# Spreading the MLP's last product evenly over the attention units, and normalising three last units in the core

## The chip, the cores and the metric

The kernel runs on one core of a Trainium2 chip. The metric is the device time of one execution, in microseconds (us). Three executions of the kernel before took 214.60, 214.85 and 216.46 us; their median is 214.85 us. The profiled execution is another one: it took 215.85 us, of which 214.1 us lie between the first and the last recorded instruction (its span).

## What is computed

`x` has 2048 rows (positions) of 512 numbers, bf16. `xn` is its layer norm. Two branches start from it and meet in the last line:

```python
qkv = xn @ wqkv                       # 32 heads of width 16
# position s attends to s, s-2, ..., s-14 (8 keys, dilation 2)
s = softmax_over_8_keys(q . k / 4) @ v, heads joined, @ wo
h  = gelu(xn @ w1)                    # 512 -> 512
hs = shifted(h) @ w2                  # four column groups, shifted by +-1 and +-2 positions
x1 = xn + hs
h2 = gelu(layernorm(x1) @ w3) @ w4    # 512 -> 1376 -> 512
out = x + s * silu(x1 + h2)
```

## The kernel before, in words

Even and odd positions never attend to each other, so the rows are held as two parities `p` of 1024 rows each, in chunks `c` (0 to 3) of 512 rows and tiles of 128 rows. All engines work in the order of the source: a loop at the end of the function ties each instruction behind the one before it on its engine. So what stands late in the source waits for all that stands before it on the same engine.

**First half (up to about 107 us of the trace): the dense products.** `qk`, `w1`, `w2`, `w3` are done chunk by chunk in pairs of accumulator banks that go round the tags x, y, z (`psa`, L102). `w2(c)` (L336) makes four tiles in two halves; each half is evicted by VectorE (L348), which adds it onto `xn`. `stats(c, j, "l3")` (L208: L213, L214) takes mean and variance of one tile. `second_norm(c)` (L352) does that for the four tiles of a chunk and then `rstd` on GpSimd (L218, L219). `second_columns(c)` (L359) normalises (L229), writes the chunk to DRAM (L363) and reads it back transposed (L365) as the operand of `w3(c)` (L370, matmuls on L380).

**Second half: 17 attention units** (`order`, L56). Unit 0 takes the first rows of both parities, units 1 to 8 go through parity 0 and 9 to 16 through parity 1, 120 new rows each. Iteration `n` of the loop on L759 does, on TensorE: `scores(n)` (L556: 8 mask matmuls, 32 small ones), `weighted(n-1)` (L597: 64 small ones), `values(n+1)` (L535: 4 matmuls), in most iterations one tile of the MLP's last product, `w4_part` (L490: 11 matmuls, accumulated in bank w), and from n = 6 on one output tile, `final` (L728: 4 matmuls with `wo`). Which iterations have a `w4` tile is told by

```python
w4_at = {n: k for k, n in enumerate([*range(13), 14])}
```

so iterations 13 and 15 have none; the tiles 14 and 15 are done behind the loop (L791, L805). ScalarE makes the exponentials (L583) and copies the values (L550). VectorE copies the sums of a unit out of the accumulator (L625, L631, L632).

**Normalising.** `weighted` gives the weighted sums and, in extra columns, the denominators. Units are joined to runs (L59): unit 0 alone, pairs (1,2) to (13,14), then 15 and 16 alone, R = 10 runs. There are two ways to divide:

- *Through DRAM* (runs 0 to 7): `sums_out` (L640) sends the denominators to a small tile (`dn`, two DMAs on SP's queue, L649) and the sums to `oT`, transposed by head (eight DMAs on GpSimd's queue, L656). Two iterations later `sums_invert` (L699) takes the reciprocal (VectorE, L704) and writes it to DRAM (SP, L706), and `sums_read` (L709) reads it back spread over partitions (SP, L712), behind a wait for the write. One iteration after that, `sums_apply` (L715, VectorE L720) multiplies.
- *In the core* (the last two runs, units 15 and 16): four of the eight DMAs of `oT` go on SP's queue and four on GpSimd's. `sums_turn` (L661) transposes the denominators by 8 matmuls (L666), `sums_inverse` (L669) takes the reciprocal (VectorE, L674) and spreads it (ScalarE, L677), `sums_back` (L682) turns it back by 4 matmuls (L688), `sums_mult` (L694, VectorE L697) multiplies `oT`.

**Accumulator banks.** `layout` (L88) closes all pools of banks and opens new ones. It is called three times: for the dense products (L106), for the attention (L488: s = 4 banks for scores, o = 2, w = 1, b = 1) and behind the last unit (L793: f, g, h, i in place of s; o, w and b again). The first matmul into a newly opened bank waits for the last readers of what was closed with it.

**The end** (L783 to L814): scores and weights of the last unit, the two runs that are normalised in the core, `w4` tiles 14 and 15, and the output tiles 2 to 7 of parity 1. `final` multiplies the product by the gate on VectorE (L742, L744) and adds `x` on GpSimd, or on VectorE for the two last (L745); the last tile is done in two halves that are stored on two queues (L747).

Of the kernel before, what the change touches and what calls it, by code (L numbers as in the profile page):

```python
# [9 lines left out]
ALU = mybir.AluOpType  # L10
# [5 lines left out]
def kernel(  # L16
# [13 lines left out]
    pe, dve, act, pool, sp = nc.tensor, nc.vector, nc.scalar, nc.gpsimd, nc.sync  # L30
# [8 lines left out]
    NF = (F + P - 1) // P  # L39
# [5 lines left out]
    TPC = CH // P  # L45
# [10 lines left out]
    order = [(None, 0)] + [(p, u) for p in range(2) for u in range(NU)]  # L56
    NN = len(order)

    runs = [(0, 0)] + [(a, a + 1) for a in range(1, NN - 2, 2)] + [(a, a) for a in range(NN - 2, NN)]  # L59

    xv = A_x.flatten_outer_dims().rearrange("(m two) d -> two m d", two=2)
    ov = out.flatten_outer_dims().rearrange("(m two) d -> two m d", two=2)
# [22 lines left out]

    banks = {}

    def layout(**tags):  # L88
        if "stack" in banks:
            banks["stack"].close()  # L90
        banks["stack"] = ctx.enter_context(ExitStack())
        for tag, n in tags.items():
            ps = banks["stack"].enter_context(tc.tile_pool(name=f"ps_{tag}", bufs=1, space=bass.MemoryType.PSUM))
            banks[tag] = (ps, n)

    def pst(tag, name):
# [6 lines left out]
        turn["a"] += 1  # L103
        return pst("xyz"[turn["a"] % 3], name)

    layout(x=2, y=2, z=2, w=1, b=1)  # L106


    xn = [bigt([P, M // P, D], f"xn{p}") for p in range(2)]
# [223 lines left out]
            q, s = p, (-1 if g == 2 else 1)  # L333
        return hT[q][:, g, 1 + m0 + s : 1 + m0 + s + P]

    def w2(c):  # L336
        p, k = c // 2, c % 2
        for h in range(TPC // 2):
            pt = psa("w2_ps")
            for j in range(2):  # L340
                m0 = k * CH + (2 * h + j) * P
                for g in range(ND):
                    pe.matmul(  # L343
                        pt[:, j, :], lhsT=w2_src(p, g, m0), rhs=w2_sb[:, g, :],
                        start=(g == 0), stop=(g == ND - 1),
                    )
            xs = xn[p][:, k * TPC + 2 * h : k * TPC + 2 * h + 2, :]
            dve.tensor_tensor(out=xs, in0=pt, in1=xs, op=ALU.add)  # L348

    x1nTs = {}  # L350

    def second_norm(c, between=None):  # L352
        for j in range(TPC):
            if j == 2 and between is not None:
                between()
            stats(c, j, "l3")
        rstd(c, 0, TPC, "l3")

# [112 lines left out]
    qk(3)  # L471
    second_columns(0)
    w1(3)
    w2(1)
    second_norm(1, lambda: w2(2))
    second_columns(1)
    second_norm(2)
    w3(0)
# [6 lines left out]
    w3(3)  # L485


    layout(s=4, o=2, w=1, b=1)  # L488

    def w4_part(t, lo, hi, tag="w"):  # L490
        c, jj = t // TPC, t % TPC
        if lo == 0:
            banks["w4", t] = pst(tag, "w4_ps")[:, 0, :]
        pt = banks["w4", t]
        for ft in range(lo, hi):
            fs = P if ft < NF - 1 else FL
            pe.matmul(  # L497
                pt, lhsT=h3[c][:fs, ft, jj * P : (jj + 1) * P], rhs=w4_sb[:fs, ft, :],
                start=(ft == 0), stop=(ft == NF - 1),
            )  # L500
        if hi == NF:
            x_i = x_tile(c, jj)
            dve.tensor_tensor(out=x_i, in0=pt, in1=x_i, op=ALU.add)  # L503
            gates.append(t)
# [135 lines left out]
    def sums_out(i):  # L640
        _, a, b, _, rw, parts = run_of(runs[i][0])
        w = orw[i]
        for p, _, _, _ in parts:
            if p not in oT:
                oT[p] = (midt if p == 0 else bigt)([P, ND, M], f"oT{p}")
        if i < R - 2:
            dn = small.tile([P, H * rw // P], BF16, name="dn", tag="dn")
            for j in range(2):
                sp.dma_start(out=dn[P // 2 * j : P // 2 * (j + 1), :], in_=w[DH : P : 32, ND * j : ND * (j + 1), :])  # L649
            rden[i] = dn  # L650
        for p, q0, c, nq in parts:
            for jj in range(2):
                for cg in range(4):
                    hh = 4 * jj + cg
                    q = pool if i < R - 2 else (sp, pool)[hh % 2]
                    q.dma_start(  # L656
                        out=oT[p][DH * hh : DH * (hh + 1), :, q0 : q0 + nq],
                        in_=w[32 * cg : 32 * cg + DH, ND * jj : ND * jj + ND, c : c + nq],
                    )

    def sums_turn(i, tag):  # L661

        w = orw[i]
        pt = pst(tag, "dt_ps")[:, 0, 0:H].rearrange("p (g c) -> p g c", c=4)
        for g in range(2 * ND):
            pe.matmul(pt[0:QU, g, :], lhsT=w[:, g, :], rhs=ident[:, DH::32], start=True, stop=True)  # L666
        rden[i] = pt
# [31 lines left out]
    def sums_invert(i):  # L699
        _, a, b, _, rw, parts = run_of(runs[i][0])  # L700
        dn = rden[i]
        rb = small.tile([P, H * rw // P], BF16, name="rb", tag="rb")
        with nc.allow_low_precision("bf16 weights"):
            dve.reciprocal(out=rb, in_=dn)  # L704
        rden_d = dram.tile([8, ND * rw], BF16, name=f"rden_d{i}")
        sp.dma_start(out=rden_d.rearrange("h (a m) -> (h a) m", a=P // 8), in_=rb)  # L706
        rden[i] = rden_d

    def sums_read(i):  # L709
        _, a, b, _, rw, parts = run_of(runs[i][0])  # L710
        rr = orw[i].rearrange("p g q -> p (g q)")[:, 0 : ND * rw]
        sp.dma_start(out=rr, in_=rden[i].unsqueeze(1).to_broadcast([8, DH, ND * rw]))  # L712
        rden[i] = rr

    def sums_apply(i):  # L715
        _, a, b, _, rw, parts = run_of(runs[i][0])
        rr = rden.pop(i).rearrange("p (s q) -> p s q", s=ND)
        for p, q0, c, nq in parts:
            o = oT[p][:, :, q0 : q0 + nq]
            dve.tensor_tensor(out=o, in0=o, in1=rr[:, :, c : c + nq], op=ALU.mult)  # L720
# [7 lines left out]
    def final(p, i, tag="b", add=pool, parts=1, tags=None):  # L728
        t = 2 * TPC * p + i
        g_i = x_tile(t // TPC, t % TPC)  # L730
        x_o = xo[p, i & ~1][:, i % 2, :]
        for k in range(parts):
            cs = slice(k * D // parts, (k + 1) * D // parts)
            pt = pst(tag if tags is None else tags[k], "wo_ps")[:, 0, cs]
            for dt in range(ND):
                pe.matmul(  # L736
                    pt, lhsT=oT[p][:, dt, i * P : (i + 1) * P], rhs=wo_sb[:, dt, cs],
                    start=(dt == 0), stop=(dt == ND - 1),
                )
            sg = fin.tile([P, D], BF16, name="sg", tag="f")[:, cs]  # L740
            if t in twice:
                dve.scalar_tensor_tensor(out=sg, in0=pt, scalar=2.0, in1=g_i[:, cs], op0=ALU.mult, op1=ALU.mult)  # L742
            else:
                dve.tensor_tensor(out=sg, in0=pt, in1=g_i[:, cs], op=ALU.mult)  # L744
            add.tensor_tensor(out=x_o[:, cs], in0=sg, in1=x_o[:, cs], op=ALU.add)  # L745
            if parts > 1:
                (sp, act)[k % 2].dma_start(out=ov[p, i * P : (i + 1) * P, cs], in_=x_o[:, cs])  # L747

# [4 lines left out]
            )  # L753

    final_at = {n: divmod(n - 6, 8) for n in range(6, 16)}
    w4_at = {n: k for k, n in enumerate([*range(13), 14])}
    W4 = len(w4_at)
    values(0)
    for n in range(NN - 1):  # L759
        scores(n)  # L760
        for i, (a, b) in enumerate(runs):
            if b == n - 2:
                sums_invert(i)
                sums_read(i)
        if n > 0:
            weighted(n - 1)
        gate_tanh()
        exps(n)
        values(n + 1)
        gate_mult()  # L770
        for i, (a, b) in enumerate(runs):
            if b == n - 3 and i < R - 4:
                sums_apply(i)
        if n in w4_at:
            w4_part(w4_at[n], 0, NF)
        if n in final_at:
            final(*final_at[n], "b" if n in w4_at else "w")
        if n % 2 == 0 and n >= 2:
            load_xo((n - 2) // 8, (n - 2) % 8)
        if n - 1 in final_at and n % 2 == 0:  # L780
            p, i = final_at[n - 1]
            store(sp, p, i - 1)
    scores(NN - 1)  # L783
    load_xo(1, 6)
    store(sp, 1, 0)
    weighted(NN - 2, lambda: sums_invert(R - 3))
    sums_read(R - 3)
    exps(NN - 1)
    act.preload_act_table_set("silu_and_others")
    sums_apply(R - 4)  # L790
    w4_part(W4, 0, NF, "b")  # L791
    weighted(NN - 1, eng=act)
    layout(f=1, g=1, h=1, i=1, o=2, w=1, b=1)  # L793
    sums_turn(R - 2, "w")
    sums_inverse(R - 2)
    gate_silu()
    final(1, 2, "f")
    final(1, 3, "g")
    sums_turn(R - 1, "h")
    sums_inverse(R - 1)  # L800
    store(sp, 1, 2)
    sums_back(R - 2, "i")
    sums_mult(R - 2)
    sums_apply(R - 3)
    w4_part(W4 + 1, 0, NF, "w")  # L805
    gate_silu()
    sums_back(R - 1, "b")
    sums_mult(R - 1)
    final(1, 4, "f")
    final(1, 5, "g")  # L810
    store(sp, 1, 4)
    final(1, 6, "h", dve)
    store(act, 1, 6, 1)
    final(1, 7, None, dve, 2, "iw")  # L814


    prev = {}
# [37 lines left out]
```

## Time and profile before

| | |
|---|---|
| median of three executions | 214.85 us |
| profiled execution | 215.85 us |
| its span | 214.1 us |
| TensorE busy | 198.0 us (92%) |
| VectorE busy | 121.2 us (57%) |
| ScalarE busy | 113.1 us (53%) |
| GpSimd busy | 84.5 us (39%) |
| mean granted TensorE clock | 0.971 |
| instruction blocks fetched on queue q8 | 21 packets, 0.34 MB |

Times in the trace count from the start of the span. A line of the chain of waits has a start, a length and what filled it; "issue" is time in which the engine waited for nothing that the profile shows. A line of the timeline has start, length, engine, source line and operation; in square brackets stands how long the engine sat idle before it and what ended that.

### The profile page before, as it was taken

To read this page: it belongs to the slowest core of one execution; us is meant where nothing else is said; L and a number is where in the kernel's file an instruction comes from. 1 tells how busy PE (TensorE), PEld (TensorE's weight loads), DVE (VectorE), ACT (ScalarE), POOL (GpSimd) and SP (SyncE) were. 2 spreads that over 40 slices of the span, in tenths; PEclk is the share of its full clock that TensorE was granted. 3 is DMA by queue.
4 is the path that set the end of the run, shared out by engine and by line. 5 is a ranking of instruction groups with operands and counts; after the bars stand their busy time and mean duration, and the time that the engine had idled before them with its cause. 6 is when DMAs were issued, how large, how long until landed. Compare 5 with 4: busy or idle time off the path is not lost.

```text
span 214.1 us, 6299 instructions
## 1 busy us (share of the span) xinstructions
PE 198.0 (92%) x2678; PEld 103.2 (48%) x2678; DVE 121.2 (57%) x248; ACT 113.1 (53%) x118; POOL 84.5 (39%) x165
## 2 busy tenths in 40 slices
PE   7899999999999989999999999999999988786930
PEld 2688745444444434444455555555555544433520
DVE  5789786186187793000016647876777684653760
ACT  3379767529405415665686656555555563734200
POOL 4136708902002202000007772465565646693440
PEclk9999999999999999999999999999999999966995
DMA  5964260391340466600001143242525252543230
GB/s 149 340 200 123 61 232 25 90 346 57 114 82 0 138 169 142 142 0 2 0 3 18 26 119 104 51 115 60 139 41 157 44 153 49 164 138 76 66 99 2
DMA packets 29708, 21.60 MB, mean 101 GB/s; under 512 B 13584, under 2 KB 29168, under 8 KB 29680
## 3 DMA queue, kind: packets, MB, share of 16 engines
q1 hardware_dynamic: 26640, 18.99, 30.9%
q0 software_dynamic: 2752, 2.01, 4.8%
q8 instruction: 21, 0.34, 0.7%
q10 hardware_dynamic: 288, 0.20, 0.3%
q14 instruction: 7, 0.06, 0.1%
HBM read 12.53 MB, written 4.31 MB: 79 GB/s over the span
## 4 chain that ended last, share of the span: by engine, by line
PE 82%; DVE 6%; DMA 4%; issue 2%; POOL 1%; ACT 0%; DVEq 0%; ACTq 0%
PE w_ps L497 18%; PE w_ps L380 13%; PE qk_ps L287 13%; PE v_ps L549 7%; PE wo_ps L736 7%; PE w_ps L320 6%; PE o_ps L610 5%; PE w_ps L343 3%; PE s_ps L564 3%; PE s_ps L575 2%; DMA x1nT<-x1n_dram 2%; PE tr_ps L267 2%; DVE xn L348 2%; DMA x1n_dram<-xn 1%; DVE l3s L213 1%
## 5 line engine op out<-in xcount | busy, mean ns | idle before, releaser
L656 POOL DMA_DIRECT2D oT<-orw x80 | 40.4, 513 | 46.1 <-DVE orw L618 31.2
L497 PE MATMUL w_ps<-w_sb,h3T 128*128 128x512 bf16 (+1 forms) x176 | 42.0, 389 | 0.0
L380 PE MATMUL w_ps<-x1nT,w_sb 128*128 128x512 bf16 (+1 forms) x176 | 38.3, 379 | 0.7 <-DMA x1nT<-x1n_dram 0.7
L385 ACT ACTIVATE h3T<-w_ps 128x1024 bf16<-128x1024 f32 x20 | 20.5, 1024 | 26.4 <-PE w_ps L380 26.4
L583 ACT ACTIVATE prob<-s_ps 128x2048 bf16<-128x2048 f32 x17 | 31.8, 1871 | 3.0 <-PE s_ps L575 2.5
L503 DVE TENSOR_TENSOR xn<-w_ps,xn 128x512 bf16<-128x512 f32 x16 | 11.0, 690 | 39.0 <-PE w_ps L497 39.0
L287 PE MATMUL qk_ps<-xnT,wqk_sb 128*128 128x256 bf16 (+1 forms) x192 | 29.3, 308 | 0.5 <-DVE xnT L271 0.5
L380 PEld LDWEIGHTS <-w_sb 128*128 128x128 bf16 (+1 forms) x176 | 17.5, 100 | 21.3 <-DMA x1nT<-x1n_dram 1.1
L497 PEld LDWEIGHTS <-h3T 128*128 128x128 bf16 (+1 forms) x176 | 17.4, 100 | 21.4 <-issue 1.9
L745 POOL TENSOR_TENSOR xo<-sg,xo 128x512 bf16<-128x512 bf16 x14 | 16.1, 1157 | 20.8 <-DVE sg L744 20.6
L287 PEld LDWEIGHTS <-wqk_sb 128*128 128x128 bf16 x192 | 18.5, 98 | 10.3 <-DMA wqk_sb<-in_A_wqkv_dram 0.5
L522 ACT ACTIVATE sig<-xn 128x512 bf16<-128x512 bf16 x14 | 8.8, 630 | 27.4 <-DVE xn L503 27.4
L294 ACT ACTIVATE qT<-qk_ps,sel 128x1024 bf16<-128x1024 f32 x16 | 16.7, 1112 | 6.3 <-PE qk_ps L287 6.3
L625 DVE CAST orw<-o_ps 128x896 bf16<-128x896 f32 x15 | 16.2, 1078 | 6.8 <-PE o_ps L610 6.8
L736 PE MATMUL wo_ps<-wo_sb,oT 128*128 128x512 bf16 (+1 forms) x68 | 17.1, 389 | 0.0
L549 PE MATMUL v_ps<-wv_sb,xnT 128*128 128x512 bf16 x64 | 16.6, 381 | 0.0
L610 PE MATMUL o_ps<-prob,v_aug 64*32 64x64 bf16 x1088 | 12.0, 196 | 3.2 <-issue 3.2
L320 PE MATMUL w_ps<-xn2T,w_sb 128*128 128x512 bf16 x64 | 14.6, 379 | 0.0
L343 PE MATMUL w_ps<-w_sb,hT 128*128 128x512 bf16 x64 | 14.3, 379 | 0.0
L218 POOL TENSOR_SCALAR l3r<-l3m 128x4 f32<-128x4 f32 x4 | 0.9, 228 | 33.7 <-DVE l3m L214 33.7
L348 DVE TENSOR_TENSOR xn<-w_ps,xn 128x1024 bf16<-128x1024 f32 x8 | 9.6, 1217 | 6.1 <-PE w_ps L343 6.1
L610 PEld LDWEIGHTS <-v_aug 64*32 64x32 bf16 x1088 | 9.6, 89 | 5.1 <-issue 3.8
(82 smaller groups left out, 230.2 us busy)
## 6 DMA issues: line engine op xcount, KB each, us to landing
x1n_dram<-xn SPq DMA_DIRECT2D x4, 512.0 KB
xo<-in_A_x_dram SPq DMA_DIRECT2D x8, 256.0 KB
out_dram<-xo SPq DMA_DIRECT2D x7, 256.0 KB
oT<-orw POOLq DMA_DIRECT2D x56, 30.0 KB, 2.5
orw<-rden_d SPq DMA_DIRECT2D x7, 240.0 KB
xn<-in_A_x_dram SPq DMA_DIRECT2D x6, 256.0 KB
w_sb<-in_B_w_dram SPq DMA_DIRECT2D x1, 1376.0 KB
w_sb<-in_B_w_dram SPq DMA_DIRECT2D x1, 1280.0 KB
```

Of the source, the lines that this page charges most:

```text
L287: pe.matmul(pt[:, b, :], lhsT=wqk_sb[:, dt, nt * P : (nt + 1) * P], rhs=xnT[p][:, dt, ms], start=(dt == 0), stop=(dt == ND - 1),)
L294: act.activation(qT[p][:, n0 : n0 + per, e, ms], pt, AF.Identity, scale=sel[:, e : e + 1])
L320: pe.matmul(pt[:, b, :], lhsT=w1_sb[:, dt, g * P : (g + 1) * P], rhs=xn2T[:, dt, :], start=(dt == 0), stop=(dt == ND - 1),)
L343: pe.matmul(pt[:, j, :], lhsT=w2_src(p, g, m0), rhs=w2_sb[:, g, :], start=(g == 0), stop=(g == ND - 1),)
L380: pe.matmul(pt[:fs, ft % 2, :], lhsT=w3_sb[:, dt, ft * P : ft * P + fs], rhs=x1nT[:, dt, :], start=(dt == 0), stop=(dt == ND - 1),)
L385: act.activation(h3T[:, 2 * a : 2 * a + 2, :], pt, AF.Gelu_apprx_tanh)
L497: pe.matmul(pt, lhsT=h3[c][:fs, ft, jj * P : (jj + 1) * P], rhs=w4_sb[:fs, ft, :], start=(ft == 0), stop=(ft == NF - 1),)
L549: pe.matmul(vp, lhsT=xnT[p][:, dt, k0 : k0 + P], rhs=wv_sb[:, dt, :], start=first, stop=last)
L583: act.activation(pr, st.pop(n).rearrange("p r (i q) -> p r i q", q=KB), AF.Exp, scale=SCALE)
L610: pe.matmul(op[32 * cg : 32 * cg + 32, s, g * KB : (g + 1) * KB], lhsT=va[KB * s : KB * s + KB, dt * 8 + h, :], rhs=pr[KB * s : KB * s + K ...
L656: q.dma_start(out=oT[p][DH * hh : DH * (hh + 1), :, q0 : q0 + nq], in_=w[32 * cg : 32 * cg + DH, ND * jj : ND * jj + ND, c : c + nq],)
L736: pe.matmul(pt, lhsT=oT[p][:, dt, i * P : (i + 1) * P], rhs=wo_sb[:, dt, cs], start=(dt == 0), stop=(dt == ND - 1),)
```

## The change

- **Runs.** The number of runs normalised in the core becomes `NC = 3`: units 14, 15 and 16. Unit 13, which shared a run with 14, becomes a run of its own through DRAM. R becomes 11.
- **w4 tiles.** Iteration n (0 to 14) does tile n. Iteration 15 does the first 6 of the 11 matmuls of tile 15; the other 5 stand behind `scores(16)` and `weighted(15)`. None is left for the end.
- **Unit 14's division.** `sums_turn` and `sums_inverse` stand in iteration 15 (the turned denominators go to bank o, which `weighted(15)` uses next), `sums_back` and `sums_mult` behind the rest of tile 15.
- **Banks.** `layout` gets a level. Bank order at the start of the attention is o, w, b, s instead of s, o, w, b, and behind the last unit only the four score banks are closed and opened again as f, g, h, i.
- **Queues.** The DMAs of `oT` of unit 14 and 15 go in turn on SP and GpSimd; those of unit 16 in turn on SP, GpSimd and ScalarE (3, 3 and 2).
- **Second norm of chunk 1.** The statistics of its four tiles now stand behind the halves of `w2(1)` and `w2(2)`: one behind the first half of `w2(1)`, two behind its second half, one behind the first half of `w2(2)`. Before, `w2(2)`'s two evictions stood between the second and the third.
- **End.** The order of the last output tiles is mixed anew with the divisions; the addition of tile 6 stands behind tile 7; its store goes on SP's queue.

```diff
+    NC = 3
+    runs = [(0, 0)] + [(a, a + 1) for a in range(1, NN - NC - 1, 2)] + [(a, a) for a in range(NN - NC - 1, NN)]
...
-    def layout(**tags):
-        if "stack" in banks:
-            banks["stack"].close()
-        banks["stack"] = ctx.enter_context(ExitStack())
+    def layout(level, **tags):
+        if level in banks:
+            banks[level].close()
+        banks[level] = ctx.enter_context(ExitStack())
...
-    w2(1)
-    second_norm(1, lambda: w2(2))
+    w2(1, {0: [(1, 0)], 1: [(1, 1), (1, 2)]})
+    w2(2, {0: [(1, 3)]})
+    rstd(1, 0, TPC, "l3")
...
-    layout(s=4, o=2, w=1, b=1)
+    layout("low", o=2, w=1, b=1)
+    layout("high", s=4)
...
-        if i < R - 2:
+        if i < R - NC:
...
-                    q = pool if i < R - 2 else (sp, pool)[hh % 2]
+                    q = pool if i < R - NC else (sp, pool)[hh % 2] if i < R - 1 else (sp, pool, act)[hh % 3]
...
-            if b == n - 3 and i < R - 4:
+            if b == n - 3:
                 sums_apply(i)
-        if n in w4_at:
-            w4_part(w4_at[n], 0, NF)
+        w4_part(n, 0, NF if n < NN - 2 else CUT)
+        if n == NN - 2:
+            sums_turn(R - 3, "o")
+            sums_inverse(R - 3)
         if n in final_at:
-            final(*final_at[n], "b" if n in w4_at else "w")
+            final(*final_at[n])
...
-    weighted(NN - 2, lambda: sums_invert(R - 3))
-    sums_read(R - 3)
+    weighted(NN - 2)
+    sums_apply(R - 4)
     exps(NN - 1)
     act.preload_act_table_set("silu_and_others")
-    sums_apply(R - 4)
-    w4_part(W4, 0, NF, "b")
+    w4_part(NN - 2, CUT, NF)
+    sums_back(R - 3, "b")
+    sums_mult(R - 3)
     weighted(NN - 1, eng=act)
-    layout(f=1, g=1, h=1, i=1, o=2, w=1, b=1)
-    sums_turn(R - 2, "w")
+    layout("high", f=1, g=1, h=1, i=1)
+    final(1, 2, "f")
+    sums_turn(R - 2, "g")
     sums_inverse(R - 2)
+    final(1, 3, "h")
+    store(sp, 1, 2)
+    sums_turn(R - 1, "i")
+    sums_inverse(R - 1)
     gate_silu()
-    final(1, 2, "f")
-    final(1, 3, "g")
-    sums_turn(R - 1, "h")
-    sums_inverse(R - 1)
-    store(sp, 1, 2)
-    sums_back(R - 2, "i")
+    final(1, 4, "w")
+    sums_back(R - 2, "b")
     sums_mult(R - 2)
-    sums_apply(R - 3)
-    w4_part(W4 + 1, 0, NF, "w")
-    gate_silu()
-    sums_back(R - 1, "b")
+    final(1, 5, "f")
+    store(sp, 1, 4)
+    sums_back(R - 1, "g")
     sums_mult(R - 1)
-    final(1, 4, "f")
-    final(1, 5, "g")
-    store(sp, 1, 4)
-    final(1, 6, "h", dve)
-    store(act, 1, 6, 1)
+    last = final(1, 6, "h", None)
     final(1, 7, None, dve, 2, "iw")
+    last(dve)
+    store(sp, 1, 6, 1)
```

## The prediction

> **What bounds the kernel now.** I read the page first: TensorE is busy 92% of the span, so the question is where it is not. The page's clock row and queue list:
>
> ```profile
> PEclk9999999999999999999999999999999999966995
> ...
> q8 instruction: 21, 0.34, 0.7%
> ```
>
> The clock is full except in two slices near 190 us; instructions come in 21 blocks of 16 KB. Next the chain of waits, in order of time:
>
> ```profile
> 72.47 4.44 DMA x1nT<-x1n_dram
> ...
> 76.95 28.66 PE w_ps L380 x132
> ...
> 175.96 1.31 issue
> 177.26 0.55 PE o_ps L610 x48
> ...
> 185.76 0.47 PE o_ps L610 x35
> 186.23 1.87 issue
> 188.11 0.40 PE o_ps L610 x22
> 188.51 3.85 PE w_ps L497 x11
> ...
> 194.60 0.93 PE dt_ps L666 x8
> 195.53 3.06 PE wo_ps L736 x8
> ...
> 207.14 0.29 DVE xo L745
> ```
>
> The reader is to see five losses. (1) `w3(1)` starts at 76.95, behind a transpose, though `w2(3)` ended at 76.30 (timeline: 72.68 + 3.62): 0.65 us. (2) and (3) 1.31 and 1.87 us in the midst of `weighted`, waiting for nothing. (4) A `w4` tile takes 3.85 us; all others take 2.38. Eight `wo` matmuls take 3.06; elsewhere four take 0.86. (5) `dt_ps` waits. The last two are in the stretches and the timeline:
>
> ```profile
> 187.84:191.25 3.41, 3.14 (x36) 1.29 (x37) 2.43 (x5) 1.38 (x2) 2.98 (x5) 0.50 0.37 106
> ```
>
> ```profile
> 191.38 3.43 SPq L656 DMA_DIRECT2D oT<-orw  x4
> ...
> 194.60 0.93 PE L666 MATMUL dt_ps<-ident,orw 128*120 128x4 bf16 x8 [1.63 <-DVE orw L632]
> ```
>
> The clock (0.50, last but two) is halved in the 3.41 us behind the 1.87 us gap, and again from 194.67 to 198.08, behind the wait of 1.63. That wait is for VectorE's last sum of unit 16, though `dt_ps` turns unit 15: the reopened bank held it.
>
> **What the gaps (2), (3) are.** From one to the other TensorE issues 48+4+11+4+40+64+4+4+40+35 = 254 matmuls, each with a weight load, and 4 waiting instructions: 512, two blocks of 256. Both gaps are at a block's end. By the packet records the next block is fetched only when the last one has begun, and is used 1.31 to 1.43 us after it has landed. From a block's beginning to the next one's readiness passed 3.5 us (177.26: fetch 1.14 later, lasting 0.99, plus 1.37), 4.65 (172.61 to 177.26), 5.43 (182.67 to 188.10) and 6.4 (188.10: fetch 3.49 later, lasting 1.56, plus 1.35); the long ones follow a load, a store and a read of SP together. An iteration with a `w4` tile lasts 5.47 us for 246 instructions and hides this. Iterations 13 and 15 have none, last 3.09 us, and the gap follows each.
>
> The Trainium skill (Runtime: NRT & Kernel Launch, Instruction fetch mechanics) has the blocks of 256, but says that crossing one is "mostly hidden". The trace has 3.18 us of it unhidden. By the page the gaps would have another cause and stay: the third rival's time.
>
> **Part by part**, on the clock of before (unit 13 begins at 172.03); the first half's gain is taken off at the end.
>
> *Second norm of chunk 1.* VectorE (timeline): evictions 1.11 apart, a pair of statistics 0.81. Now: eviction 58.21, statistics to 60.14, eviction 61.25, two pairs to 62.90, eviction 64.04, last pair aggregated at 64.94, against 66.62 before. `rstd`, normalising and the two DMAs follow 1.68 earlier, so the transpose lands at 75.2, before 76.30. The second eviction of `w2(2)` moves to 66.07; its bank is needed by `w3(0)`'s third pair at 63.19 + 2 x 1.73 = 66.65. Gain 0.65; what is late next is nothing, TensorE is gapless from there.
>
> *Iterations 13 to 15.* All now take what the others take: unit 14 begins at 177.50, unit 15 at 182.97. Iteration 15: 0.65 scores, 0.61 weights, 0.97 values, 6/11 of 2.38 = 1.30, turning of unit 14 0.40 (L666's later row), output tile 0.86, so scores(16) at 187.76, weighted(15) at 188.41. Then 1.08 for five matmuls, 0.21 for turning back, 190.31. `weighted(16)` waits for VectorE to empty bank o (1.03+0.22+0.23 and hops behind 189.02): 190.75 to 191.4, against 193.07.
> Blocks now begin 10, 16 and 20 instructions into weighted(13), (14), (15), and at the first weight of output tile (1,2). The spans between are 5.5, 4.8 and 2.9 us. So gap (2) goes. Gap (3) becomes 4.8 against 3.5 to 6.4: 0 to 1.6, by its own row 5.43: 0.6. A new one of 0.6 to 3.5 comes at 191.4. TensorE has 5.5 us of work from there until tile 7's halves can start at 200.3 (below), so 3.4 us of waits cost nothing there.
>
> *Bank o in iteration 15.* `weighted(15)` now waits for the reciprocal of unit 14 on VectorE, behind unit 13's reciprocal, the copies of unit 14, the gate (0.68) and `sums_apply` (0.65): done at 188.0, needed at 188.41. Nothing, with 0.4 to spare; 1 us if `dn` lands 1.4 later.
>
> *SP's queue* sets the end. The read of run 6 issues at 180.96 as before; `dn` of unit 13 (two of 0.57) behind it; the reciprocal 2.8 after its issue (174.88 to 177.70), 184.4; the write at 184.8; the read 2.7 behind that (178.26 to 180.96), to 188.1. `oT` of unit 14, four issues (3.43, row above): 191.5; the last small writes of before landed 1.3 us after their issue: 192.8. VectorE stands at `sums_mult(14)` then, with unit 16's addition queued behind: 0.62+0.46, 193.9, so turn(16), GpSimd's and ScalarE's `oT` issues wait for that too. SP goes on: load and store 0.8, `oT` of 15 3.43, three of unit 16 2.6: 198.3, landed 199.6. The multiplication of unit 16: 200.3. Then VectorE: tile 6 0.69, two halves of tile 7 2 x (0.43+0.31), the last addition 2 x 0.29 by its halves' row: 203.0, with hops 203.3, against 207.43. That is 4.1 less. Loss (5) is gone with the layout; the turning of unit 14 (0.61 of TensorE) and two more ScalarE issues lie under this queue. The last store is 128 KB instead of 64, on SP: 0 to 0.3, I take 0.1.
>
> *Half clock.* 1.31 us of gap did not halve it, 1.53 did. The new gap may: 0 if not, up to two windows of 1.7 lost. With the slack of 3.4 against waits of 0.6 to 3.5: 0 to 3.4. I take 0.6, near none, since the longest fetch alone uses the slack up.
> The skill (TensorE: Matmul & The Clock Gate, Part 1) halves the clock after an idle window of about 3.4 us; this trace did it with gaps of half that. By the page the term would be 0, the time 0.6 less.
>
> **Sum**: -0.65 - 4.1 + 0.1 + 0.6 = -4.05 on the profiled span of 214.1. The profiled execution is 1.0 above the median; I put the difference on 214.85: 210.8 us.
>
> **Rivals.**
> - *Fetch and half clock take the slack*: gap of 3.5 at 191.4, one or two half windows: +2.2 to +3.4 instead of +0.6, 212.4 to 213.6, say 212.9. For: 254 small matmuls in 2.9 us is denser than anything before. Against: the 6.4 was seen once.
> - *SP lands later*: each us of `oT(14)` or `oT(16)` counts in full; 1.3 late gives 212.1. For: SP waits 2.0 for a `rden_d` write. Against: fewer bytes than before.
> - *The change doesn't do what it says*: gaps (2), (3) have another cause and stay: +1.31 in full, 1.87 and a half window against the slack, some 0.5 over what I take: 212.6.
> - *Slower*: the read of unit 13's factors on SP waits also for that unit's eight `oT` issues on GpSimd; with it `oT(14)`, VectorE's `sums_mult(14)` and all behind. Such a wait was 4.2 us at most in this trace. One for one from 192.8; even at 197; over 1% slower from 199 on.
>
> **Chances.** Forecast 0.61 (own range 209.2 to 212.0), fetch and clock 0.17, SP 0.09, gaps stay 0.07, slower 0.06. One per cent, about what a measurement can tell from no change, is 2.1 us: 212.7 and 217.0. Faster: 0.61 + 0.09 + half of 0.17 + a little of 0.07 = 0.80; within 1%: 0.14; slower: 0.06. Range 208.9 (SP's last writes prompt, no half clock: 1.9 less) to 213.5 (fetch rival's upper half left out).
>
> **What would show it.** No wait before `w3(1)`; no "issue" in weighted(13); `dt_ps` without VectorE's wait; 2.38 for all `w4` tiles; a gap in front of tile (1,2); VectorE waiting for `oT` at `sums_mult(14)` and (16). Wrong: a gap over 3.5 us at 191, half clock in the last tiles, or the end set by something other than SP's small writes.

## The result, and the profile after

The kernel after took 211.82 us (median of 11 executions, 210.77 to 213.68), the kernel before 214.56 us beside it (11 executions, 213.91 to 217.08). The ratio is 0.9885 with a 95% interval of 0.9842 to 0.9928. On another chip it was 0.984 (0.9805 to 0.9875; first experiment below). The change makes the kernel faster by a good one per cent; the forecast of 210.8 us was 1.0 us too low and its range holds the result. Where some executions of a kernel took over 1.5% more than its fastest, the medians and ratios in this text are of the others.

The profiled execution of after took 213.52 us, its span is 211.8 us. Where its time lies against before, with a second profiled execution of the same kernel:

| us from the start of the span | before | after | after, again |
|---|---|---|---|
| first `scores` | 106.53 | 107.09 | 105.64 |
| `scores(13)` | 171.96 | 173.12 | 171.53 |
| end of VectorE's last piece | 207.43 | 205.89 | 204.25 |
| span | 214.1 | 211.8 | 210.1 |
| `scores(13)` to VectorE's end | 35.47 | 32.77 | 32.72 |

The stretch that the change rearranges is 2.7 us shorter in both than in this execution of before. The rows ahead of it differ by as much as 1.45 us between two executions of one kernel (in after the first statistics of `x` start at 3.71 us and the granted clock from 8 to 12 us is 0.62, in the second execution 3.06 and 1.00), so a single span doesn't tell the parts of this change from one another; below, stretches are compared within an execution, and medians where there are several executions. The stretch itself isn't free of this either: the kernel with the moved statistics alone has the same code from `scores(13)` on as before, and there it takes 34.16 us in its profile, 1.3 less than in before's (why is said under "Half clock").

The page of after, its clock row and the instruction queue:

```profile
PEclk9799999999999999999999999999999999999997
...
q8 instruction: 21, 0.34, 0.6%
```

Of before's two dim slices near 190 us none is left; the number of instruction blocks is the same. The timeline of after where `w3(1)` follows `w2(3)`:

```profile
77.53 8.80 PE L383 MATMUL w_ps<-x1nT,w_sb 128*128 128x512 bf16 x40
```

No bracket stands behind the line: `w3(1)` doesn't wait for its transpose any more. From the start of `w2(3)` (74.07) it is 3.46 us, against 4.27 before (72.68 to 76.95): 0.81 less. TensorE's waits from 170 us on (us in total, times, longest):

```profile
PE wo_ps L741 <- DVE oT L702: 1.8, 2, 1.3
PE dt_ps L671 <- DVE orw L637: 1.5, 1, 1.5
PE wo_ps L741 <- DMA oT<-orw: 1.0, 1, 1.0
```

The 1.31 and 1.87 us of "issue" inside `weighted` are gone. A wait of `dt_ps` of about the old size is still there, but it is another one: before, it was the reopened bank behind unit 16; now it is unit 14's turning in iteration 15. The timeline shows what it waits for, and how the end goes:

```profile
183.13 0.61 SPq L717 DMA_DIRECT2D orw<-rden_d  x1
183.80 1.12 SPq L654 DMA_DIRECT2D dn<-orw  x2
...
187.76 0.34 DVE L709 RECIPROCAL rb<-dn 128x30 bf16<-128x30 bf16 x1 [2.82 <-DMA dn<-orw]
...
189.48 0.61 PE L671 MATMUL dt_ps<-ident,orw 128*120 128x4 bf16 x8 [1.51 <-DVE orw L637]
...
194.85 5.31 SPq L661 DMA_DIRECT2D oT<-orw  x7
...
195.58 0.56 PEld L741 LDWEIGHTS <-oT 128*128 128x128 bf16 x4 [0.89 <-issue]
```

VectorE stood idle for 2.82 us until unit 13's denominators (`dn`, issued on SP at 183.80 behind a read) had landed. Its copies of unit 14 (from 188.01 on) stand behind that reciprocal, and the turning behind the copies. Later SP issues seven small `oT` writes without a pause, 0.76 us each. The 0.89 us of "issue" before the first weight of output tile (1,2) is, by the count of instructions, the block that begins there. The chain of waits of after goes from one of these places to the other:

```profile
184.38 3.28 DMA dn<-orw
...
199.04 2.94 DMA oT<-orw
...
202.71 0.67 DVE oT L702
```

So a transfer, `dn`, begins the last stretch, and SP's writes end it; in the second execution too.

### The profile page after: what moved, and what is told of

Read it like the earlier page. It is cut to its first block, busy times and chain, and to the rows that moved or that the text cites. A ratio compares the mean times of both kernels' runs of the same rounds, so it can differ in the third digit from the quotient of the medians.

```text
span 211.8 us, 6335 instructions
## 1 busy us (share of the span) xinstructions
PE 194.8 (92%) x2664; PEld 103.6 (49%) x2690; DVE 121.8 (58%) x251; ACT 113.8 (54%) x120; POOL 86.0 (41%) x168
## 4 chain that ended last, share of the span: by engine, by line
PE 83%; DVE 4%; DMA 4%; issue 2%; SPq 2%; ACT 1%; DVEq 0%; ACTq 0%
PE w_ps L383 18%; PE w_ps L502 16%; PE qk_ps L289 14%; PE w_ps L322 7%; PE v_ps L554 7%; PE w_ps L346 6%; PE o_ps L615 4%; PE wo_ps L741 4%; PE s_ps L569 2%; PE s_ps L580 2%; PE tr_ps L269 2%; SPq L661 2%; DMA dn<-orw 2%; DMA oT<-orw 1%; DMA xn<-in_A_x_dram 1%
## 5 line engine op out<-in xcount | busy, mean ns | idle before, releaser
L661 POOL DMA_DIRECT2D oT<-orw x83 | 41.9, 513 | 46.7 <-DVE orw L623 30.6
L502 PE MATMUL w_ps<-w_sb,h3T 128*128 128x512 bf16 (+1 forms) x175 | 40.6, 379 | 0.2 <-issue 0.2
L289 PE MATMUL qk_ps<-xnT,wqk_sb 128*128 128x256 bf16 (+1 forms) x190 | 30.5, 320 | 0.6 <-DVE xnT L273 0.5
L527 ACT ACTIVATE sig<-xn 128x512 bf16<-128x512 bf16 x15 | 9.4, 629 | 29.7 <-DVE xn L508 29.7
L289 PEld LDWEIGHTS <-wqk_sb 128*128 128x128 bf16 x192 | 19.3, 102 | 10.9 <-DMA wqk_sb<-in_A_wqkv_dram 0.5
L741 PE MATMUL wo_ps<-wo_sb,oT 128*128 128x512 bf16 (+1 forms) x67 | 16.2, 365 | 3.2 <-DVE oT L702 1.8
L554 PE MATMUL v_ps<-wv_sb,xnT 128*128 128x512 bf16 x48 | 15.7, 382 | 0.9
L749 DVE TENSOR_TENSOR sg<-wo_ps,xn 128x512 bf16<-128x512 f32 x15 | 10.4, 690 | 3.9 <-PE wo_ps L741 2.9
```

The costliest lines, as they stand in the source:

```text
L289: pe.matmul(pt[:, b, :], lhsT=wqk_sb[:, dt, nt * P : (nt + 1) * P], rhs=xnT[p][:, dt, ms], start=(dt == 0), stop=(dt == ND - 1),)
L502: pe.matmul(pt, lhsT=h3[c][:fs, ft, jj * P : (jj + 1) * P], rhs=w4_sb[:fs, ft, :], start=(ft == 0), stop=(ft == NF - 1),)
L554: pe.matmul(vp, lhsT=xnT[p][:, dt, k0 : k0 + P], rhs=wv_sb[:, dt, :], start=first, stop=last)
L661: q.dma_start(out=oT[p][DH * hh : DH * (hh + 1), :, q0 : q0 + nq], in_=w[32 * cg : 32 * cg + DH, ND * jj : ND * jj + ND, c : c + nq],)
L741: pe.matmul(pt, lhsT=oT[p][:, dt, i * P : (i + 1) * P], rhs=wo_sb[:, dt, cs], start=(dt == 0), stop=(dt == ND - 1),)
```

## The experiments

Each kernel was timed in five rounds against the kernel before, except where another number is given. "Before" is the base of the kernels that do one part alone, "after" of those that undo or alter one. The kernels made from before ran on one chip, after once more and three of those made from it (old places of the tiles, late reciprocal, fourth unit) on a second. The other four ran on two more chips without after beside them; they are compared with after by their ratios to before. A profile is of one execution, and where that took over 1 us more than the kernel's median, the text gives its time.

### The kernel after once more

No edit; it is the base of the comparisons on that chip.

> The changed kernel once more, as it is, on the chip of the next three: ratio 0.984 to 0.993 to the kernel before. In its profile turning unit 14's denominators again waits 1 to 2 us for VectorE, which waits for dn of unit 13.

211.85 us (211.31 to 212.13) against 215.87: ratio 0.984 (0.9805 to 0.9875). The median repeats to 0.03 us; it is the kernel before that reads 214.6 to 215.9 from one comparison to the next. In the profile the turning of unit 14 waits 1.7 us for VectorE, and VectorE 2.75 for `dn`, as expected.

### The moved statistics alone

```diff
...
-    w2(1)
-    second_norm(1, lambda: w2(2))
+    w2(1, {0: [(1, 0)], 1: [(1, 1), (1, 2)]})
+    w2(2, {0: [(1, 3)]})
+    rstd(1, 0, TPC, "l3")
```

> The kernel before with the moved statistics of chunk 1 alone. The wait before w3(1) goes: 0.65 to 0.8 us less, ratio 0.996 to 0.997. Rival, the transpose is not what w3(1) waits for last or the moved evictions cost as much: ratio 1.000.

214.02 us, ratio 0.9952 (0.9917 to 0.9987). From the start of `w2(3)` to `w3(1)` it is 3.45 us in its profile. This part pays by itself (0.13 to 0.83%), and what the forecast gave it lies in that interval (0.65 us is 0.3%).

### The even w4 tiles alone

```diff
-    w4_at = {n: k for k, n in enumerate([*range(13), 14])}
-    W4 = len(w4_at)
+    CUT = 6
...
-        if n in w4_at:
-            w4_part(w4_at[n], 0, NF)
+        w4_part(n, 0, NF if n < NN - 2 else CUT)
...
-    w4_part(W4, 0, NF, "b")
+    w4_part(NN - 2, CUT, NF)
...
-    w4_part(W4 + 1, 0, NF, "w")
-    gate_silu()
```

> The kernel before with the w4 tiles alone spread (one in each iteration, tile 15 cut 6 + 5), runs, banks and second norm as before. Fetch theory: both gaps go (1.31 + 1.87) and with the second the half clock behind it (1.5); the wait of dt_ps for unit 16 stays (1.5) and a gap up to 3.5 may come at the end of weighted(16): 2.5 to 4 us less, ratio 0.982 to 0.988. Rival, the gaps have another cause: ratio 0.995 to 1.005, gaps still there.

215.26 us (three rounds), ratio 1.0009 (0.9975 to 1.0043): no gain, though the gaps shrink. So neither side of the expectation came: the gaps were as the fetch theory had them, the time as the rival had it. The chain of waits of this kernel says what took their place:

```profile
188.14 0.82 issue
...
196.25 3.58 DMA orw<-rden_d
200.66 4.46 PE wo_ps L736 x12
```

The first gap is gone and one of 0.82 is left of the second. But now TensorE reaches the output tiles of units 13 and 14 before their factors have come back from DRAM (landed 199.83), and these tiles run at a lower clock behind the wait (4.46 us for 12, against 2.60 in before). Seventeen `w4` matmuls moved from the end into the middle don't help when the division is late at the end.

### The bank order alone

```diff
...
-    layout(s=4, o=2, w=1, b=1)
+    layout("low", o=2, w=1, b=1)
+    layout("high", s=4)
...
-    layout(f=1, g=1, h=1, i=1, o=2, w=1, b=1)
+    layout("high", f=1, g=1, h=1, i=1)
```

> The kernel before with the new bank layout alone. If the wait of dt_ps was the reopened bank: it goes, 1.5 us, and with it perhaps the half clock from 194.67 on (1.4): 0.5 to 2.9 less, ratio 0.987 to 0.998. Rival, VectorE and the DMAs end the tail anyway: ratio 0.998 to 1.002.

214.80 us, ratio 0.9998 (0.9961 to 1.0034): no gain that this interval could tell from none. The wait of `dt_ps` for VectorE is gone (1.63 in before); what stands at `dt_ps` now is 0.6 us of "issue" in the midst of unit 16's turning. The page's clock row has no dim slice near the tail. The gaps stay (1.59 and 2.15 us of "issue"), and the chain of this kernel shows the same successor:

```profile
195.97 3.19 DMA oT<-orw
199.16 0.65 DVE oT L721
```

L721 is the multiplication of units 13 and 14 again, for which `wo` waits 1.3 us.

### 48 TensorE instructions more in the warm-up

```diff
+    for i in range(24):
+        pe.matmul(wm[:, 0, 0:32], lhsT=ones_bf[:], rhs=ones_bf[:, 0:32], start=True, stop=True)
```

This adds 24 tiny matmuls (with their weight loads, 48 instructions) some 180 us ahead of the gaps and leaves nothing out.

> The kernel before with 24 tiny matmuls (48 TensorE instructions) more in the warm-up, nothing else. If the two gaps are the fetch of the next block of 256 instructions, both stay (1 to 2.5 us each) but sit 48 instructions earlier in the program: the first no longer behind 16 matmuls of weighted(13) but 8 matmuls before the end of scores(14), the second behind 11 matmuls of weighted(15) instead of 35. If they belong to the work of these units (data, a bank, a semaphore), they stay behind 16 and behind 35 matmuls.

213.8 us, one execution, so only its places are read and not its time. The chain of waits of this kernel:

```profile
184.70 0.17 PE o_ps L612 x11
184.86 1.40 issue
...
189.33 0.60 PE o_ps L612 x63
189.94 0.90 issue
```

In before, the second gap stood behind 35 of the 64 matmuls of `weighted(15)`; here it stands behind 11: exactly 24 matmuls earlier. A wait for data would stay with its instruction; this one stays with the count of instructions, and one block (256) later, before the last matmul of `weighted(16)`, the next gap appears. By the count the first gap should now stand in `scores(14)`. It isn't seen there; only `weighted(13)` takes 0.94 instead of 0.61, and why wasn't followed. So the expectation held for one gap of two. That (3) of the prediction is the end of an instruction block is shown; that (2) is one rests on the count and on its having left its place.

The Trainium skill (Runtime: NRT & Kernel Launch, Instruction fetch mechanics) says that crossing a block is "mostly hidden". Here 1.31 and 1.87 us weren't hidden in before, and 1.40 and 0.90 weren't in this kernel.

### After with the old places of the w4 tiles

```diff
-        w4_part(n, 0, NF if n < NN - 2 else CUT)
+        if n in w4_at:
+            w4_part(w4_at[n], 0, NF)
...
-    w4_part(NN - 2, CUT, NF)
+    w4_part(14, 0, NF)
...
-    final(1, 5, "f")
+    w4_part(15, 0, NF, "w")
+    gate_silu()
+    final(1, 5, "h")
...
```

> The changed kernel with the old places of the w4 tiles (none in iterations 13 and 15, tiles 14 and 15 behind the loop), all else as changed. Theory: the gap in weighted(13) comes back (1 to 1.8 us) and one of 0.5 to 2.5 in weighted(15), so 1.5 to 3.5 us more than the changed kernel: near the kernel before. Rival, the runs and the banks bring the gain and the place of the tiles none: within 0.5 us of the changed kernel.

215.18 us, ratio 0.9982 (0.9942 to 1.0022): the gain goes. But not by the gaps that were expected back: in the profile (216.40 us) 0.39 us of "issue" stands in `weighted(13)` and none in `weighted(15)`. The timeline of this kernel:

```profile
187.15 0.96 PE L671 MATMUL dt_ps<-ident,orw 128*120 128x4 bf16 x8 [3.30 <-DVE orw L637]
...
191.54 3.47 PE L502 MATMUL w_ps<-w_sb,h3T 128*128 128x512 bf16 x11
```

Without a tile to cover them, the waits for units 13 and 14 grow: 3.30 us at the turning, and what stands behind it runs at a lower clock (the granted clock is 0.50 from 187 to 191.5 us; the `w4` tile takes 3.47 us against 2.54 where the clock is full).

### After with two units in the core, as before

```diff
-    NC = 3
+    NC = 2
...
-        if n == NN - 2:
-            sums_turn(R - 3, "o")
-            sums_inverse(R - 3)
...
-    weighted(NN - 2)
-    sums_apply(R - 4)
+    weighted(NN - 2, lambda: sums_invert(R - 3))
+    sums_read(R - 3)
...
-    sums_back(R - 3, "b")
-    sums_mult(R - 3)
...
+    sums_apply(R - 3)
     final(1, 4, "w")
```

> The kernel after with only the last two units in the core, as before the change: units 13 and 14 are one run through DRAM again, and its multiplication stands in front of output tile (1,4). The spread w4 tiles, the bank order, the moved statistics and the new order of the end stay. Theory (the spread tiles only move the limit to the way through DRAM of units 13 and 14, and the third run in the core is what takes that away): the chain of the end runs through the read of that run's factors and the multiplication behind it, in front of tile (1,4), and the gain falls to about what the moved statistics give by themselves, a ratio to the kernel before of 0.993 to 1.000. Rival (tiles, banks and the new order of the end are enough together): no wait for the read at the multiplication, a ratio of 0.984 to 0.990.

216.28 us, ratio 1.0056 (1.0022 to 1.0091): slower than before, more clearly than the theory had it, and far from the rival. From its profile (217.97 us) the chain and the largest wait:

```profile
197.55 3.75 DMA orw<-rden_d
...
202.14 1.90 PE wo_ps L741 x4
```

```profile
PE wo_ps L741 <- DVE oT L725: 3.9, 1, 3.9
```

Here is the price of the way through DRAM at the end, bare: TensorE, which has no `w4` tile left to put there, stands still for 3.9 us, and then needs 1.90 us for four matmuls that take 0.86 elsewhere (the granted clock is 0.50 from 196 to 204 us, so already ahead of this wait).

### The wait of iteration 15: the reciprocal behind it

```diff
-            if b == n - 2:
+            if b == n - 2 and n < NN - 2:
...
+        if n == NN - 2:
+            sums_invert(R - 4)
+            sums_read(R - 4)
```

The division of unit 13 is moved behind `gate_mult` of iteration 15, so that the copies of unit 14 don't stand behind `dn`.

> The changed kernel with the reciprocal of unit 13 (and its write and read) moved behind the copies and the gate of unit 14 in iteration 15, nothing else. Theory: the copies no longer wait for dn, the wait of dt_ps in iteration 15 (1.5 us) goes, SP's read of unit 13 comes at most 0.5 later: 0.7 to 1.5 us less than the changed kernel. Rival, SP's small writes of units 14 to 16 alone set the end: within 0.4 us of the changed kernel or later by the shift of the read.

212.75 us, ratio 0.988 (0.9842 to 0.9918): not better than after. The wait leaves iteration 15 and comes back at the turning of unit 16, by the waits and the chain of its profile (214.57 us):

```profile
PE dt_ps L671 <- DVE orw L637: 2.5, 1, 2.5
```

```profile
192.90 2.93 DMA orw<-rden_d
195.95 0.12 DVE oT L725
```

VectorE now waits 4.15 us for unit 13's factors in front of unit 16's addition, and the turning of unit 16 waits for that.

### The wait of iteration 15: dn on another queue

```diff
-                sp.dma_start(out=dn[...], in_=w[...])
+                (pool if i == R - 4 else sp).dma_start(out=dn[...], in_=w[...])
```

> The changed kernel with the two dn DMAs of unit 13 issued on GpSimd's queue, ahead of its oT DMAs, instead of on SP's queue behind the read of units 11 and 12; nothing else. Theory, dn of unit 13 is late because of what stands before it on SP: the reciprocal of unit 13 starts at least 1 us sooner after scores(15), the wait of dt_ps in iteration 15 shrinks from 1.5 to 1.7 to under 0.7, and 0.5 to 1.5 us are gained on the changed kernel. Rival, the DMA engines are full then whatever the queue, or SP's small writes at the end bind: the wait stays over 1.2 us, or it goes and the time stays within 0.3 us of the changed kernel.

212.28 us, ratio 0.9877 (0.9833 to 0.9922): not better either. But in its profile the wait of `dt_ps` in iteration 15 falls from 1.5 to 0.2 us, so `dn`'s place on SP's queue was its cause. The timeline shows where the time went:

```profile
181.32 4.10 POOL L661 DMA_DIRECT2D oT<-orw  x8
...
183.09 0.33 DVE L709 RECIPROCAL rb<-dn 128x30 bf16<-128x30 bf16 x1
183.45 0.33 SPq L711 DMA_DIRECT2D rden_d<-rb  x1
...
188.04 0.62 SPq L717 DMA_DIRECT2D orw<-rden_d  x1
```

The reciprocal comes 0.79 us after `scores(15)` (182.30) instead of 3.7, and the write follows at once. SP's read of the factors is issued at 188.04 all the same, 4.6 us behind that write, and SP's waits put 3.8 us of that down to `oT` transfers. By the code, the read overwrites the tile from which unit 13's eight transfers on GpSimd's queue (issued until 185.42) read. `oT` of unit 14 on SP stands behind it, from 188.72 on. This is the mechanism of the prediction's fourth rival; here it takes back what the earlier `dn` gave.

### A fourth unit in the core

```diff
-        if i < R - NC:
+        if i < R - 4:
...
+        if n == NN - 3:
+            sums_turn(R - 4, "o")
+            sums_inverse(R - 4)
...
+    sums_back(R - 4, "b")
+    sums_mult(R - 4)
     weighted(NN - 2)
-    sums_apply(R - 4)
```

> The changed kernel with unit 13 too normalised in the core (turned and inverted in iteration 14, turned back behind scores(16)): its dn, its write and its read leave SP's queue, TensorE gets 0.6 us more of turning. Theory, unit 13's way through DRAM is what holds VectorE in iteration 15 and SP behind it: 1 to 2.5 us less than the changed kernel. Rival, TensorE and the fetch of its instructions bound the tail: 0 to 0.8 us more than the changed kernel.

211.89 us, ratio 0.9857 (0.981 to 0.9904): the same as after, and not the 1 to 2.5 us less of the theory. The chain of this kernel goes by ScalarE's queue:

```profile
194.41 0.71 ACTq L661
...
195.16 1.92 ACTq L661
```

Its two `oT` issues take 2.6 us, and the spreading of unit 15's reciprocals (197.13) stands behind them.

### No oT on ScalarE's queue

```diff
-  ... else (sp, pool)[hh % 2] if i < R - 1 else (sp, pool, act)[hh % 3]
+  ... else (sp, pool)[hh % 2]
```

> The changed kernel with the oT DMAs of unit 16 on SP and GpSimd alone (4 and 4 in place of 3, 3 and 2 on ScalarE). Theory 1, ScalarE's two issues (1.3 to 2.7 us) hold the spreading of the factors of units 15 and 16 and are worth more than SP's eighth issue: 0.2 to 0.8 less than the changed kernel. Theory 2, SP's writes end the tail: 0.6 to 0.9 more.

211.81 us, ratio 0.9854 (0.9813 to 0.9894): the same as after, and neither the gain of the first theory nor the loss of the second. Its chain ends on SP's writes, as in after:

```profile
198.14 1.85 DMA oT<-orw
```

### Both, with unit 13's multiplication behind unit 15's copies

The two edits before this, and `sums_mult(R - 4)` put where `sums_apply(R - 4)` stands in after.

> The changed kernel with unit 13 normalised in the core too, its multiplication behind VectorE's copies of unit 15, and no oT DMA on ScalarE. If the waits seen so far are the whole of it (dn and the way through DRAM, VectorE's wait for oT of unit 13 in front of the copies, ScalarE's issues): 1 to 2.5 us less than the changed kernel. If TensorE's fetch and VectorE bound the rest: within 0.8 us of it.

211.66 us, ratio 0.9833 (0.9794 to 0.9871): the lowest median of all, by 0.2 us under after, which the intervals don't tell apart. The next wait is in its timeline:

```profile
198.48 0.69 DVE L749 TENSOR_TENSOR sg<-wo_ps,xn 128x512 bf16<-128x512 f32 x1 [1.61 <-POOL xo L750]
```

VectorE waits for one of GpSimd's additions to give back a buffer.

## Why the prediction held, step by step

**Front (-0.65).** Right in mechanism and size: 0.81 in the profile, and 0.13 to 0.83% by the kernel with that part alone.

**The gaps (2) and (3).** Right. They are ends of instruction blocks (shown for (3) by the 48 instructions that moved it by 24 matmuls, by the count for (2)), with the even tiles one goes and the other shrinks to 0.82, in after both are gone, and the new one comes at output tile (1,2): 0.7 us in one profiled execution of after, 0.9 to 1.0 in the other, near the lower end of 0.6 to 3.5. Between the blocks' beginnings and readiness passed 3.0 to 3.7 us in the tail of after, reckoned from the packet records as in the prediction; the 6.4 wasn't seen again there. The rival "gaps stay" and the fetch rival are out.

**Half clock (+0.6).** Not seen in after: the granted clock is 1.00 from 184 to 204 us in both profiled executions, so the term was 0 there. In the kernel with `dn` on another queue it is 0.51 from 198 to 200 us, behind a wait of 1.1 us, so it isn't 0 for every tail of this kind. And the reading on which the term rests, "1.31 us of gap did not halve it, 1.53 did", is no bound. In the profile of the moved statistics alone the gap (3) is 1.88 us long, as in before, but the clock stays 1.00 behind it (187.7 to 191.2 us; the `w4` tile takes 2.48), and behind the 2.15 us of the bank order alone it does too. The first of these two has the clock row

```profile
PEclk9999999999999999999999999999999999998895
```

The length of a gap alone doesn't tell whether the clock halves; what else does wasn't followed. Loss (4) of the prediction is one of the execution that was profiled, and not of each. Of 29 executions of before on one chip, 16 had a mean granted clock of 0.977 or more and took 214.1 to 215.2 us, and 13 had 0.973 or less and took 215.3 to 217.6; the profiled one (0.971, 215.85 us) is of the second kind.

The skill's rule (TensorE: Matmul & The Clock Gate, Part 1: halved after an idle window of about 3.4 us) gives 0 for after as well; before's rows, halved behind 1.53 and 1.87 us, are still not what that rule says.

**Banks.** Right that the hand-over wait goes (the kernel with that part alone).

**The tail (-4.1).** Here lies the error: 2.7 was measured, so 1.4 are missing. VectorE ended at 204.73 on the prediction's clock (1.16 us under the trace of after, by the start of unit 13) and not at 203.3. The step that failed is "The read of run 6 issues at 180.96 as before; `dn` of unit 13 (two of 0.57) behind it; the reciprocal 2.8 after its issue (174.88 to 177.70), 184.4". On that clock the read issued at 181.97, `dn` at 182.64, and the reciprocal came at 186.60, 3.96 after it and not 2.8: 2.2 late in all. Of these 1.0 us came from the read: run 6's reciprocal came 0.5 later, behind VectorE's sum of the new `w4` tile, and the read 3.28 instead of 2.70 behind the write. Another 1.1 came from `dn`'s landing. Its neighbours on the queue (a read just ahead, a load and a store behind) are what differs from the row that I took; that they are the cause wasn't tried by itself. The text had the consequence ready ("Nothing, with 0.4 to spare; 1 us if `dn` lands 1.4 later") and took the wrong side of it. What follows in the chain is the same delay handed on: turning (1.5 of waiting), `weighted(15)`, unit 15's copies, SP's seven writes (begun 1.4 late, then 0.7 faster than reckoned, the last landing 1.8 behind its issue instead of 1.3), and the multiplication of unit 16 at 201.55 instead of 200.3.

The 2.7 itself is against an execution of before whose clock halved twice in that stretch. Against the 34.16 us of the moved statistics alone, where it halved once (near 194 to 198 us), 1.4 remain. The medians (2.74 less in all, some 0.8 of it the front's) put the tail's gain between the two, near 1.9. That the forecast came within 1.0 us is in part luck: the 0.6 for the clock, which wasn't needed, made up for part of the 1.4, while a difference reckoned on an execution 1.3 us over the median (215.85 against 214.56) was put on that median.

**SP sets the end.** Right for after: its chain ends on SP's writes of `oT`. But taking the wait away isn't worth what it is long. Five kernels that remove or move a link (the reciprocal's place, `dn`'s queue, unit 13 in the core, ScalarE's issues, the two last together) all stay within 0.9 us of after, and each shows another wait next: VectorE's factors, SP's read, ScalarE's issues, SP's writes, GpSimd's additions. From that I take it that at the end of this kernel several chains are nearly equally long; which of them holds the last microsecond wasn't settled.

**What the parts are worth together.** The forecast added the parts; the runs show that the tail's parts don't add:

| kernel | ratio to before |
|---|---|
| moved statistics alone | 0.9952 |
| even tiles alone | 1.0009 |
| banks alone | 0.9998 |
| all but the even tiles | 0.9982 |
| all but the third unit in the core | 1.0056 |
| all, two chips | 0.9885, 0.984 |

Even tiles bring TensorE to the last output tiles sooner, and take away the tile that stood there as cover; the factors through DRAM are then late by as much. The third unit in the core brings the factors sooner, and without the even tiles its turning waits 3.3 us. Take away either and the gain is gone, so the gain of the tail is that of both. The third unit by itself on top of before wasn't run, nor were the new order of the end and the new queues, so what these are worth alone isn't known. The prediction's sum had no such link between its terms.

## What to carry to other kernels

When a wait is removed near the end, name the next thing that must be ready at that moment, and check the terms of a sum in pairs: two edits that are worth nothing alone can be worth 1% together. A wait in the midst of small matmuls may belong to the instruction count; shifting the count by some dummies shows it. A loss that is seen in one profiled execution may not be in the median: look whether another kernel with the same code there shows it too. A small DMA may land later where other things stand around it on its queue, so take its landing time from a row with the same neighbours, and move it along with all that its engine does before it.

## What the runs showed of the chip

- Small issues on SP cost what their count makes them: seven of 16x4x120 took 5.31 us in after, 0.76 each, and the last landed 1.8 us behind. The Trainium skill (DMA: Bandwidth & Descriptors, Issuing engines are not separate DMA queues) calls the sequencer's time to start a DMA "usually small relative to the DMA itself". Here one was about a quarter of the 2.94 us from the start of the last issue to its landing, and the seven together were most of the row.
- A pair of such issues on ScalarE took 2.6 us with a fourth unit in the core (0.71 and 1.92) and 1.36 with two units in the core, while SP and GpSimd issued theirs.
- Iteration 6, which the change leaves alone, took 5.98 and 5.88 us in the two profiled executions of after, and 5.47 or 5.48 in before and in four of the eight kernels made from after (5.68 to 5.86 in the rest). In the first execution of after VectorE waited 1.92 us there for a read of factors from DRAM, against 1.23 in before, and ScalarE's copy of the values came 0.35 us too late for the first output tile. Why that read landed later wasn't followed; 0.4 to 0.5 us is lost there in both profiled executions of after.
